# Second MoE of an attention + MoE + MoE kernel: six of eight token blocks taken in pairs, with seven products for eight

## The chip, the core and the metric

The kernel runs on one core of a Trainium2 chip, as one launch. The metric is the device time of that launch in microseconds (us). Three timed runs of the kernel before gave 904.86, 905.05 and 905.75 us; their median, 905.05 us, is the time to compare with.

## What is computed

Gated linear attention over 4 batches, 8 heads, 768 steps, then a MoE with a SiLU gate, then a second MoE with a maximum over three products. All arrays are float32.

```python
def _moe2_ref(x, w1, w2, w3, w_out) -> np.ndarray:      # x: 3072 tokens x 384; w1..w3: 384 x 768; w_out: 768 x 384
    h = np.maximum(np.maximum(x @ w1, x @ w2), x @ w3)
    return (h @ w_out).astype(np.float32)

def reference(**kwargs):
...
    attn_out = _attn_ref(**attn_kwargs)
    B, H, S, D = attn_out.shape
    x = np.ascontiguousarray(attn_out.transpose(0, 2, 1, 3)).reshape(B * S, H * D)
    x = _moe_ref(x=x, **moe_kwargs)
    return _moe2_ref(x=x, **moe2_kwargs)
```

Only the second MoE (`_moe2_ref`) is computed in another way after the change.

## The kernel before

**Numbers.** Every float32 operand of a MoE product is kept as two parts, a high and a low one (names that end in h and l), and a product of two 128-row tiles is three TensorE matmuls: high by high, high by low, low by high. One matmul here has 128x128 stationary weights and 384 moving columns.

**Stages.** Attention (24 tiles of 128 tokens) is worked into the first MoE, whose output y1 goes to HBM (`y1_scr`). The second MoE reads y1 back in 8 blocks of 384 tokens (`yf`, L919), splits it (`yh` L931 on ScalarE, `yl` L934 on VectorE), and goes through 6 tiles f of the 768 hidden columns per block. One such (block, f) is a slot z, 48 in all. In a slot, `p` 0 to 2 are the products with w1, w2, w3 (L769, 9 matmuls each, into PSUM banks 3, 4, 5); ScalarE copies the first out (`cp`, L951); VectorE takes the maximum with the second and the third (`m`, L954, two instructions); the hidden tile is split into high (`hh2`, L958, ScalarE) and low (`hl2`, L962, VectorE); `s2` (L969, 9 matmuls) multiplies it with w_out into banks 0 to 2. So a slot has 36 matmuls and three VectorE instructions. After a block's six slots ScalarE copies the banks out and they are stored (`ev2`, L995, L996).

**Order.** All work of the stages is given as parts to a planner (class `Order`): a name, an engine, an estimated cost, a due time, the parts that it needs. A list schedule over these numbers sets the order in which each engine's instructions are written out; the engines then run their own lists in order and wait on semaphores. `MM` is the planner's cost of nine matmuls, for the first MoE's parts too. The weights of the second MoE (`w0h` to `w2l`, `wo2h`, `wo2l`) are fetched and split during the end of the first MoE and the start of the second.

In the printed code, `slots` are the (block, f) of the first MoE (gate and value products L769, second product L816), and `wvh`, `wvl`, `woh`, `wol` are its weights, which the second MoE no longer needs.

## Time and profile before

| | us |
|---|---|
| median of three timed runs | 905.05 |
| the profiled execution's own time | 905.86 |
| its span, first to last instruction | 903.7 |
| TensorE (PE) busy | 886.8 (98%) |
| VectorE (DVE) busy | 530.5 (59%) |
| ScalarE (ACT) busy | 350.4 (39%) |
| second MoE, from its first product to the last matmul | 589.7 to 897.3 |

The profiled execution took 2.2 us more than its span, and is 0.81 us over the median. PE is TensorE's matmuls, PEld its weight loads (beside them), DVE VectorE, ACT ScalarE, SP the queue that issues the DMAs. Matmuls are pipelined: each is shown some 0.34 us long while the next begins after about half of that.

### The profile page before, as it was taken

What the parts mean: (1) busy time and instruction counts of PE and PEld (TensorE: products, weight loads), DVE (VectorE), ACT (ScalarE), POOL (GpSimd) and SP (SyncE); (2) the same over time, 40 slices, a digit from 0 to 9 for tenths busy, and PEclk for the clock granted to TensorE, in tenths of its full rate; (3) what the DMA queues carried; (4) which work ended last, traced back from release to release, by engine and by line L of the source; (5) the groups of instructions that cost most, each with busy time, mean ns of one, the idle gap of its engine ahead of it and who ended that gap; (6) DMA issues with size and microseconds to landing.
All of it is one profiled execution on the core that took longest, in us unless ns stands there. A gap on an engine that the chain in (4) does not pass through costs nothing.

```text
span 903.7 us, 16408 instructions
## 1 busy us (share of the span) xinstructions
PE 886.8 (98%) x6527; PEld 864.9 (96%) x6527; DVE 530.5 (59%) x1063; ACT 350.4 (39%) x898; POOL 22.5 (2%) x66
## 2 busy tenths in 40 slices
PE   7999999999999999999999999999999999999997
PEld 6889999999999999999999999999999999999996
DVE  8999999987666666666663377483332323323221
ACT  4578775333333223233233277561221212212121
POOL 1000000000000000000000000000000000000000
PEclk9999999999999999999999999999999999999999
DMA  9845654343223223223201145140110100101000
GB/s 196 190 114 159 193 168 131 101 123 84 58 57 85 57 58 84 58 58 81 61 10 45 36 131 164 39 140 17 37 53 1 53 27 27 53 1 53 1 27 30
DMA packets 106243, 69.17 MB, mean 77 GB/s; under 512 B 49200, under 2 KB 103856, under 8 KB 106160
## 3 DMA queue, kind: packets, MB, share of 16 engines
...
q14 instruction: 30, 0.25, 0.1%
...
## 4 chain that ended last, share of the span: by engine, by line
PE 89%; DVE 4%; DMA 3%; SPq 2%; ACT 1%; issue 1%; DVEq 0%; ACTq 0%
PE bank L769 56%; PE bank L816 15%; PE bank L969 8%; PE bank L653 2%; PE bank L691 2%; PE bank L685 2%; DMA raw<-in_moe_w_val_dram 1%; PE bank L676 1%; DVE cv_t L59 1%; DVE cv_t L60 1%; SPq L551 1%; PE bank L776 1%; PE bank L725 1%; SPq L562 1%; PE bank L646 1%
## 5 line engine op out<-in xcount | busy, mean ns | idle before, releaser
L954 DVE TENSOR_TENSOR sg<-sg,bank 128x384 f32<-128x384 f32 x96 | 53.2, 554 | 173.0 <-PE bank L769 172.7
L802 DVE TENSOR_TENSOR sg<-sg,bank 128x384 f32<-128x384 f32 x96 | 52.8, 550 | 94.5 <-PE bank L769 93.1
L806 ACT ACTIVATE hh<-sg 128x384 fp32r<-128x384 f32 x96 | 50.0, 520 | 134.4 <-DVE sg L802 134.3
L769 PE MATMUL bank<-xh,wgh 128*128 128x384 f32 x288 | 100.7, 350 | 0.0
L816 PE MATMUL bank<-hh,woh 128*128 128x384 f32 x288 | 98.3, 341 | 0.0
L769 PE MATMUL bank<-xl,wgh 128*128 128x384 f32 x288 | 97.2, 337 | 1.2 <-DVE xl L736 1.2
L816 PE MATMUL bank<-hl,woh 128*128 128x384 f32 x288 | 96.9, 336 | 1.3 <-DVE hl L810 1.3
L769 PE MATMUL bank<-xh,wgl 128*128 128x384 f32 x288 | 97.3, 338 | 0.1
L769 PE MATMUL bank<-xh,wvh 128*128 128x384 f32 x288 | 97.0, 337 | 0.0
L769 PE MATMUL bank<-xh,wvl 128*128 128x384 f32 x288 | 96.5, 335 | 0.0
L816 PE MATMUL bank<-hh,wol 128*128 128x384 f32 x288 | 96.4, 335 | 0.0
L769 PE MATMUL bank<-xl,wvh 128*128 128x384 f32 x288 | 96.3, 334 | 0.0
L958 ACT ACTIVATE hh<-sg 128x384 fp32r<-128x384 f32 x48 | 25.2, 525 | 160.0 <-DVE sg L954 160.0
L810 DVE TENSOR_TENSOR hl<-sg,hh 128x384 fp32r<-128x384 f32 x96 | 53.3, 555 | 31.3 <-ACT hh L806 31.3
L799 ACT ACTIVATE sg<-bank 128x384 f32<-128x384 f32 x96 | 46.7, 487 | 52.3 <-PE bank L769 51.3
L816 PEld LDWEIGHTS bank<-hl,woh 128*128 128x128 f32 x288 | 54.3, 188 | 2.4 <-DVE hl L810 2.3
L816 PEld LDWEIGHTS bank<-hh,woh 128*128 128x128 f32 x288 | 54.2, 188 | 1.8
L769 PEld LDWEIGHTS bank<-xl,wgh 128*128 128x128 f32 x288 | 54.5, 189 | 1.5 <-DVE xl L736 1.5
L769 PEld LDWEIGHTS bank<-xh,wgh 128*128 128x128 f32 x288 | 54.4, 189 | 1.5
L769 PEld LDWEIGHTS bank<-xh,wgl 128*128 128x128 f32 x288 | 54.5, 189 | 0.5 <-DVE wgl L380 0.5
L769 PEld LDWEIGHTS bank<-xh,wvh 128*128 128x128 f32 x288 | 54.1, 188 | 0.5 <-DVE sg L802 0.3
L816 PEld LDWEIGHTS bank<-hh,wol 128*128 128x128 f32 x288 | 54.2, 188 | 0.0
...
## 6 DMA issues: line engine op xcount, KB each, us to landing
...
```

What stands on the lines that cost most here:

```text
L653: nc.tensor.matmul(self.sc[i][:, pr, :], self.kT[lo:hi, pr, :], self.qT[lo:hi, pr, :], start=True, stop=True)
L685: nc.tensor.matmul(self.y[tk, 2 * pr:2 * pr + 2, :].rearrange("p a d -> p (a d)"), self.qT[:, pr, tk], Sds[self.s][:, pr, :], start=True, ...
L691: nc.tensor.matmul(self.y[tk, 2 * pr + i, :], at[i][:, pr, tk], vt[:, 2 * pr + i, :], start=not self.c, stop=True, skip_group_check=True,)
L769: nc.tensor.matmul(ps, w_[:, kt, col], m_[:, kt, :], start=i == 0, stop=i == 3 * KT - 1)
L799: nc.scalar.activation(hid[s], banks[3][:, :NB], AF.Silu)
L802: nc.vector.tensor_tensor(hid[s], hid[s], banks[4][:, :NB], ALU.mult)
L806: nc.scalar.activation(hi_[s], hid[s], AF.Copy)
L810: nc.vector.tensor_tensor(lo_[s], hid.pop(s), hi_[s].bitcast(F32), ALU.subtract)
L816: nc.tensor.matmul(banks[e][:, :NB], w_[:, f, es], m_, start=f == f0 and i == 0, stop=f == f1 - 1 and i == 2)
L954: nc.vector.tensor_tensor(hid2[z], hid2[z], banks[3 + j][:, :NB], ALU.max)
L958: nc.scalar.activation(hi2[z], hid2[z], AF.Copy)
L969: nc.tensor.matmul(banks[t][:, :DM], l_[:, tsl], r_[:, f, :], start=f == 0 and i == 0, stop=f == NF2 - 1 and i == 2)
```

## The change

Blocks 0 and 1 of the second MoE stay as they were (12 slots). Blocks 2 to 7 are taken in three pairs. For a pair, a weight matrix j and two neighbouring f tiles, the hidden tiles (two f by two blocks) are a 2x2 product of tiles over three inner tiles of 128. Over inner tiles 0 and 1 that is eight products of tiles; the changed code forms sums of tiles and takes seven (a Strassen scheme). Inner tile 2 is done plainly (four products). A pair has nine such steps k (three f pairs by three j), each with seven groups X1 to X7 on PE, of 3, 3, 6, 6, 3, 6 and 6 matmuls. Groups accumulate onto what an earlier group left in the same bank, after VectorE or ScalarE has read it.

Added around the steps: nine sets of weight sums, made once on VectorE and ScalarE while blocks 0 and 1 run (`sr`, `sc`, `sh`, `sl`, then `fr`, `fh`, `fl`); four sums of y1 tiles for each pair (`t`, with splits `th`, `tl`) beside the splits of both blocks (`xh`, `xl`); in a step a copy `cp` (ScalarE), the sums `q`, `r`, and `v` 3, 2, 1 and the maxima `m` 0 to 3 (VectorE). X6 and X7 of a step are written into the next step. The hidden tiles of the pair are all kept (`hh`, `hl`), and the second product follows as parts W for six token tiles: first 12 matmuls each over the first four f, then 6 each over the last two; X6 and X7 of the last step stand behind the first W. The second product's count of matmuls does not change. Both y1 blocks of the next pair are fetched when X7 of the last step is done.

`MM` goes from 1.47 to 1.565. The core of the diff:

```diff
+    MM = 1.565
 
...
-    for blk in range(NBLK):
+
+    PLAIN = 2
+    NZ = PLAIN * NF2
+    for blk in range(PLAIN):
...
         plan.add(("s2", z), "PE", MM, due + 1.2, [("hl2", z), wts2.ready(index2["o", f]),
+                 ("X2", "sb", 1, 0) if z == NZ - 1 else None,
                  ("s2", z - 1) if z else ("s", NS - 1)] +
...
+    def whole_again(n):
+        fp, j = divmod(n, 3)
+        both = slice(2 * fp * P, 2 * (fp + 1) * P)
+        whole[n] = rt[0].tile([P, KT, 2, P], F32, name="raw", bufs=3)
+        h_, l_ = (w_[:, :, both].bitcast(F32) for w_ in w2s[j])
+        nc.vector.tensor_tensor(whole[n].rearrange("p k i f -> p k (i f)"), h_, l_, ALU.add)
+
+    def combine(n):
+        a, t = whole.pop(n), rt[0].tile([P, 5, P], F32, name="raw", bufs=3)
+        five[n] = t
+        nc.vector.tensor_tensor(t[:, 0], a[:, 0, 1], a[:, 1, 1], ALU.add)
+        nc.vector.tensor_tensor(t[:, 1], t[:, 0], a[:, 0, 0], ALU.subtract)
+        nc.vector.tensor_tensor(t[:, 2], a[:, 0, 0], a[:, 0, 1], ALU.subtract)
+        nc.vector.tensor_tensor(t[:, 3], a[:, 1, 0], t[:, 1], ALU.subtract)
+        nc.vector.tensor_tensor(t[:, 4], a[:, 2, 0], a[:, 2, 1], ALU.subtract)
+
+    def sums_high(n):
+        if not sums:
+            sums[0] = left.tile([P, KT, F1], F32R, name="wvh")
+            sums[1] = left.tile([P, KT, F1], F32R, name="wvl")
+            sums["first"] = lts[0].tile([P, 3, 2, P], F32R, name="first")
...
+        nc.vector.tensor_tensor(sum_views(n, 1), five.pop(n)[:, 1:5], sum_views(n, 0).bitcast(F32), ALU.subtract)
+
...
+    for n in range(NS1):
+        fp, j = divmod(n, 3)
+        at = NS + 3 + 0.5 * n
+        ready = [("w2", "rest", (len(chunks2) - 1) // 2 * 2), ("sl", n - 1) if n else None]
+        plan.add(("sr", n), "DVE", 1.1, at, ready, partial(whole_again, n))
+        plan.add(("sc", n), "DVE", 1.15, at, [("sr", n)], partial(combine, n))
+        plan.add(("sh", n), "ACT", 0.7, at, [("sc", n), ("s", NS - 1)], partial(sums_high, n))
+        plan.add(("sl", n), "DVE", 0.85, at + 0.05, [("sh", n)], partial(sums_low, n))
...
+        last_use = [("p", NF2 + 2 * fp + 1, j)] if fp < 2 else []
+        at = NS + 10.5 + 0.1 * n
+        plan.add(("fr", n), "DVE", 0.65, at, [("sl", NS1 - 1)] + last_use, partial(first_again, n))
...
+    def three(ps, w_, x_, start):
+
+        for i, (l, r) in enumerate(((w_[0], x_[0]), (w_[0], x_[1]), (w_[1], x_[0]))):
+            nc.tensor.matmul(ps, l, r, start=start and i == 0, stop=i == 2, skip_group_check=True)
+
+    kept = []
+    sets = (6, 7, 3), (4, 5, 0), (1, 2)
+    MM1 = MM / 3
+    last_pe = ("p", NZ - 1, 2)
+    for sb in range(1, NBLK // 2):
+        b0, b1 = 2 * sb, 2 * sb + 1
+        at0 = NS + NZ + (sb - 1) * 11.3
+        xs, T, hid3, tmp = {}, {}, {}, {}
+        A_, B_, E_ = sets
...
+        def fetch0(b0=b0, xs=xs):
+            xs["h", 0] = mp.tile([P, KT, NB], F32R, name="xh")
+            xs["l", 0] = mp.tile([P, KT, NB], F32R, name="xl")
+            nc.sync.dma_start(out=xs["l", 0].bitcast(F32), in_=y1_scr[:, :, b0 * NB:(b0 + 1) * NB])
...
+        def mixed(i, xs=xs, T=T):
+
+            b11, b21 = (xs["l", 0][:, k_, :].bitcast(F32) for k_ in (0, 1))
+            b12, b22 = (xs["f"][:, k_, :] for k_ in (0, 1))
+            T["f", i] = lts[0].tile([P, NB], F32, name="hid", bufs=7)
+            x_, y_ = {1: (b12, b11), 2: (b22, T.get(("f", 1))), 3: (b22, b12), 4: (b21, T.get(("f", 2)))}[i]
+            nc.vector.tensor_tensor(T["f", i], x_, y_, ALU.subtract)
...
+        if sb == 1:
+            free0, free1 = [("p", NF2 - 1, 2)], [("wo2 there",)]
+            free_x1, early = [("p", NZ - 1, 2)], NS + 7
+            free_t = [("sl", n) for n in range(NS1)]
...
+            free0 = free1 = free_x1 = free_t = [("X7", "sb", sb - 1, 8)]
+            early = at0 - 3
...
+        plan.add(name("yf", 0), "SP", 1.64, early, [("yst", final[0], i) for i in range(KT)] + free0, fetch0, later=2.2)
+        plan.add(name("yf", 1), "SP", 1.64, early, [("yst", final[1], i) for i in range(KT)] + free1 + [name("yf", 0)],
...
+        for i in range(1, 5):
+            plan.add(name("t", i), "DVE", 0.55, early, [name("yf", 0), name("yf", 1)] + free_t + free1, partial(mixed, i))
+            plan.add(name("th", i), "ACT", 0.5, early, [name("t", i)], partial(mixed_h, i))
...
+            def X1(ps=bank_a, w_of=w_of, x_of=x_of):
+                three(ps, w_of(0, 0), x_of(0, 0), True)
+
+            def X2(ps=bank_b, s_of=s_of, T=T):
+                three(ps, s_of(2), T[2], True)
+
+            def X3(ps=bank_c, s_of=s_of, w_of=w_of, x_of=x_of, T=T):
+                three(ps, s_of(1), T[1], True)
+                three(ps, w_of(1, 2), x_of(2, 1), False)
+
+            def X4(ps=bank_a, w_of=w_of, x_of=x_of):
+                three(ps, w_of(0, 1), x_of(1, 0), False)
+                three(ps, w_of(0, 2), x_of(2, 0), False)
+
+            def X5(ps=bank_b, s_of=s_of, T=T):
+                three(ps, s_of(3), T[3], False)
+
+            def X6(ps=bank_b, w_of=w_of, x_of=x_of, T=T):
+                three(ps, w_of(1, 1), T[4], False)
+                three(ps, w_of(1, 2), x_of(2, 0), False)
+
+            def X7(ps=bank_c, s_of=s_of, x_of=x_of):
+                three(ps, s_of(4), x_of(1, 1), False)
+                three(ps, s_of(5), x_of(2, 1), False)
...
+            x1ready = [name("xl", 1, i) for i in range(KT)]
+            pe("X1", MM1, at, old + xready + [wts2.ready(index2[j, 2 * fp]), wts2.ready(index2[j, 2 * fp + 1])], X1)
+            pe("X2", MM1, at, [name("tl", 2), ("sl", n)], X2)
+            after = [("s2", NZ - 1)] if sb == 1 and k == 0 else []
+            pe("X3", 2 * MM1, at, [name("tl", 1), ("fl", n)] + x1ready + after, X3)
+            if k:
+                for kind, cost, need, run in kept_back:
+                    pe(kind, cost, at, need, run, k=k - 1)
+            pe("X4", 2 * MM1, at, [name("cp", k)], X4)
+            pe("X5", MM1, at, [name("q", k), name("tl", 3)], X5)
+            kept_back = [("X6", 2 * MM1, [name("r", k), name("tl", 4)], X6), ("X7", 2 * MM1, [name("v", k, 3)], X7)]
...
+            plan.add(name("q", k), "DVE", 0.55, at + 0.1, [name("X2", k), name("cp", k)] +
+                     ([name("m", k - 2, 1)] if k > 1 else []), add_q)
+            plan.add(name("r", k), "DVE", 0.55, at + 0.3, [name("X5", k)] + ([name("m", k - 2, 3)] if k > 1 else []), add_r)
+            hold = [name("hl", fp - 1, i) for i in range(4)] if fp and j == 0 else []
+            plan.add(name("v", k, 3), "DVE", 0.55, at + 0.3, [name("r", k), name("X3", k)] + hold, partial(last_add, "r", bank_c, 3))
+            plan.add(name("v", k, 2), "DVE", 0.55, at + 0.9, [name("X6", k)] + hold, partial(last_add, "p", bank_b, 2))
+            plan.add(name("v", k, 1), "DVE", 0.55, at + 0.9, [name("X7", k)] + hold, partial(last_add, "q", bank_c, 1))
+            plan.add(name("m", k, 0), "DVE" if j else "ACT", 0.55, at + 0.4, [name("X4", k)] + hold +
+                     ([name("m", k - 1, 0)] if j else []), first_of)
+            for i in (3, 2, 1):
+                if j:
+                    plan.add(name("m", k, i), "DVE", 0.55, at + 0.9, [name("v", k, i), name("m", k - 1, i)], partial(most_of, i))
+                else:
...
+
+                def low(i, fp=fp, hid3=hid3):
+                    e_ = (2 * fp + i // 2) * 2 + i % 2
+                    nc.vector.tensor_tensor(
+                        stored[1][:, e_, :], hid3.pop((fp, i)), stored[0][:, e_, :].bitcast(F32), ALU.subtract
+                    )
...
+        for late in range(2):
+            for t in range(2 * TPB):
+                def second(part=late, t=t, i=out_banks[t]):
+                    wo2h, wo2l = wo2s
+                    b, tt = divmod(t, TPB)
+                    tsl = slice(tt * P, (tt + 1) * P)
+                    fs = range(4, NF2) if part else range(4)
+                    for f in fs:
+                        h_, l_ = (st[:, 2 * f + b, tsl] for st in stored)
+                        for m_, (l, r) in enumerate(((h_, wo2h), (l_, wo2h), (h_, wo2l))):
+                            nc.tensor.matmul(
+                                banks[i][:, :DM], l, r[:, f, :], start=f == 0 and m_ == 0, stop=f == NF2 - 1 and m_ == 2
...
+                    need += [name("m", 7, i) for i in range(4)] + [name("m", 8, 0)]
+                elif not late and sb == 1:
+                    need += [("ev2", PLAIN - 1, tt) for tt in range(TPB)]
+                plan.add(name("W", t, late), "PE", MM1 * (2 if late else 4), at, need + [kept[-1]], second)
...
-    plan.add("flag", "DVE", 1.5, NS + NZ - 6, [("m", NZ - 5, 1)] + [("w2", "check", i) for i in range(len(chunks2))],
+    plan.add("flag", "DVE", 1.5, NS + NZ + 20, [("W", "sb", 1, 0, 0)] + [("w2", "check", i) for i in range(len(chunks2))],
              flag)
```

**VectorE in the middle of a pair.** First the kernel before, two slots of a late block: `m`, `m`, `hl2` each.

```order
L954 TENSOR_TENSOR sg<-sg,bank_77 128x384
L954 TENSOR_TENSOR sg<-sg,bank_78 128x384
L962 TENSOR_TENSOR hl<-sg,hh 128x384
L954 TENSOR_TENSOR sg<-sg,bank_77 128x384
L954 TENSOR_TENSOR sg<-sg,bank_78 128x384
```

Then the changed kernel, second pair, around step 1: `r` and `v` 3 of step 1 (L1216, L1224), a maximum (L1230), `q` of step 2 (L1212), `v` 2 and 1 of step 1 with their maxima, `m` 0 of step 2 (L1237), `r` of step 2.

```order
L1237 TENSOR_TENSOR hid<-hid,bank_77 128x384
L1216 TENSOR_TENSOR hl<-sg,bank_78 128x384
L1224 TENSOR_TENSOR hl<-hl,bank_73 128x384
L1230 TENSOR_TENSOR hid<-hid,hl 128x384
L1212 TENSOR_TENSOR hh<-sg,bank_75 128x384
L1224 TENSOR_TENSOR sg<-sg,bank_78 128x384
L1230 TENSOR_TENSOR hid<-hid,sg 128x384
L1224 TENSOR_TENSOR hh<-hh,bank_73 128x384
L1230 TENSOR_TENSOR hid<-hid,hh 128x384
L1237 TENSOR_TENSOR hid<-hid,bank_74 128x384
L1216 TENSOR_TENSOR hl<-sg,bank_75 128x384
```

Where a slot of 36 matmuls had three VectorE instructions, a step of 33 has five (j = 0), nine (j = 1) or thirteen (j = 2, with four `hl`): 27 in three steps.

**PE at the handover from block 1 to the first pair.** Before, at the same place: the end of p 2 of a slot (w2), and then two of the next slot's products ahead of this slot's `s2`.

```order
L769 MATMUL bank_78<-xl,w2h 128x384
L769 MATMUL bank_78<-xh,w2l 128x384
L969 MATMUL bank_73<-wo2h,hh 128x384
L969 MATMUL bank_73<-wo2h,hl 128x384
L969 MATMUL bank_73<-wo2l,hh 128x384
```

(The L969 rows there are the `s2` of the slot before.) Now, with the last p 2 of block 1 in the first rows, X1 and X2 of the first step, and then the `s2` of that same slot (L972):

```order
L769 MATMUL bank_78<-xl,w2h 128x384
L769 MATMUL bank_78<-xh,w2l 128x384
L1085 MATMUL bank_79<-xh,w0h 128x384
L1085 MATMUL bank_79<-xl,w0h 128x384
L1085 MATMUL bank_79<-xh,w0l 128x384
L1085 MATMUL bank_80<-raw,wvh 128x384 x2
L1085 MATMUL bank_80<-raw,wvl 128x384
L972 MATMUL bank_73<-wo2h,hh 128x384
L972 MATMUL bank_73<-wo2h,hl 128x384
```

Six matmuls stand between a slot's last product and its own `s2`, where 27 or more stood.

**PE in the first MoE, where only `MM` differs.** Before, the transposes and scores of an attention tile (L646, L653) come right behind a second product:

```order
L816 MATMUL bank_75<-hl,woh 128x384
L816 MATMUL bank_75<-hh,wol 128x384
L646 MATMUL bank_78<-ident,kT 128x112 x4
L653 MATMUL bank_79<-qT,kT 128x128
L653 MATMUL bank_80<-qT,kT 128x128
```

Now they stand four groups of nine matmuls later, behind a value product:

```order
L769 MATMUL bank_77<-xh,wvh 128x384
L769 MATMUL bank_77<-xl,wvh 128x384
L769 MATMUL bank_77<-xh,wvl 128x384
L646 MATMUL bank_78<-ident,kT 128x112 x4
L653 MATMUL bank_79<-qT,kT 128x128
```

Up to the second MoE, PE's list differs at such places alone: this tile, one group of nine a little behind it, the parts of the next tiles up to about one tile further, and one `s2` in the first slots of the second MoE. VectorE's and ScalarE's lists differ in the same stretch, and again where the second MoE's weights are split.

## Rows read from the trace of the kernel before

**Rows 1.** The page, parts 1 and 2: busy times, tenths by slice.
```profile
PE 886.8 (98%) x6527; PEld 864.9 (96%) x6527; DVE 530.5 (59%) x1063; ACT 350.4 (39%) x898; POOL 22.5 (2%) x66
...
PE   7999999999999999999999999999999999999997
...
DVE  8999999987666666666663377483332323323221
...
PEclk9999999999999999999999999999999999999999
```
**Rows 2.** The page, part 4: the chain that ended last, by engine.
```profile
PE 89%; DVE 4%; DMA 3%; SPq 2%; ACT 1%; issue 1%; DVEq 0%; ACTq 0%
```
**Rows 3.** Windows (us, then busy and count of PE, PEld, DVE, ACT, POOL; clock).
```profile
645.38:860.40 215.02, 215.02 (x1226) 215.02 (x1225) 63.71 (x117) 47.54 (x98) 0.00 (x0) 1.00 0.09 28
```
**Rows 4.** What PE waited for, whole span: us in total, times, longest.
```profile
PE bank L816 <- DVE hl L810: 1.3, 3, 0.9
...
PE bank L769 <- DVE xl L736: 1.2, 1, 1.2
```
**Rows 5.** Groups by line in 620 to 860: busy us, mean ns, idle before.
```profile
L954 DVE TENSOR_TENSOR sg<-sg,bank 128x384 f32<-128x384 f32 x76 | 42.1, 554 | 145.1 <-PE bank L769 145.1
...
L769 PEld LDWEIGHTS bank<-xl,w2h 128*128 128x128 f32 x114 | 21.4, 188 | 0.0
...
L951 ACT ACTIVATE sg<-bank 128x384 f32<-128x384 f32 x38 | 18.7, 492 | 50.7 <-PE bank L769 50.7
L934 DVE TENSOR_TENSOR xl<-xl,xh 128x384 fp32r<-128x384 f32 x18 | 9.0, 551 | 0.0
```
**Rows 6.** Timeline of VectorE near 671 us: three instructions in a row.
```profile
671.55 1.49 DVE L934 TENSOR_TENSOR xl<-xl,xh 128x384 fp32r<-128x384 f32 x3
```
**Rows 7.** Groups of VectorE by form, other widths.
```profile
L666 DVE TENSOR_TENSOR at<-bank,mask 128x512 f32<-128x512 f32 x48 | 30.9, 684 | 15.3 <-PE bank L653 15.3
...
L626 DVE TENSOR_TENSOR Sd<-S,all 48x192 f32<-48x192 f32 x40 | 13.6, 340 | 0.3
```
**Rows 8.** Timelines of PE, DVE and ACT, 893 to 898 us.
```profile
893.53 0.34 PE L769 MATMUL bank<-xh,w2l 128*128 128x384 f32 x1
...
895.29 0.34 PE L969 MATMUL bank<-wo2h,hh 128*128 128x384 f32 x1
895.67 0.44 PE L969 MATMUL bank<-wo2h,hl 128*128 128x384 f32 x1
...
893.91 0.55 DVE L954 TENSOR_TENSOR sg<-sg,bank 128x384 f32<-128x384 f32 x1 [0.96 <-PE bank L769]
895.05 0.56 DVE L962 TENSOR_TENSOR hl<-sg,hh 128x384 fp32r<-128x384 f32 x1 [0.59 <-ACT hh L958]
...
894.50 0.53 ACT L958 ACTIVATE hh<-sg 128x384 fp32r<-128x384 f32 x1 [3.20 <-DVE sg L954]
896.32 1.56 ACT L995 ACTIVATE yo<-bank 128x384 f32<-128x384 f32 x3 [1.29 <-PE bank L969]
```
**Rows 9.** Windows: blocks 0 and 1, and a stretch of the first MoE.
```profile
589.70:666.00 76.30, 76.10 (x434) 75.75 (x433) 34.02 (x70) 26.70 (x64) 0.00 (x0) 1.00 0.18 58
...
100.00:200.00 100.00, 98.88 (x816) 95.44 (x815) 94.87 (x197) 54.89 (x152) 3.14 (x8) 1.00 0.54 147
```
**Rows 10.** DMAs: L919 to landing; two loads in flight from 589.74; rate.
```profile
DMA to landing us min/median/max: 4.2/4.5/5.0
...
589.74 0.53 SPq L919 DMA_DIRECT2D xl<-y_scr  x1
...
590.38 4.93 DMA raw<-in_moe_w_dram
...
593.70:594.70 1.00, 1.00 (x8) 1.00 (x7) 0.04 (x1) 0.48 (x2) 0.00 (x0) 1.00 1.13 393
```
**Rows 11.** Timelines of PE and DVE near 123 us, the tile of the third pair of lists.
```profile
123.08 0.55 PE L646 MATMUL bank<-ident,kT 112*128 112x112 f32 x4
123.56 1.16 PE L653 MATMUL bank<-qT,kT 48*128 48x128 f32 x16
...
125.80 1.28 DVE L666 TENSOR_TENSOR at<-bank,mask 128x512 f32<-128x512 f32 x2
```

More of the change, by code (lines that the diff above doesn't have):

```diff
@@ L770, in products @@
                 i += 1
-    MM = 1.47
+    MM = 1.565
     def fill():
@@ L859, in gla_moe_moe @@
     w2s = []
-    wo2s = []
+    wo2s, lts, stored = [], [], []
     def right():
@@ L999, in gla_moe_moe, with rows_of, sum_views, first_sum @@
                          ([] if blk else [("yst", len(passes) - 1, t)]), evacuate)
+    NS1 = 9
+    def rows_of(fp, i):
+        return cols(2 * fp + i)
+    sums = {}
+    def sum_views(n, half):
+        t = sums[half].rearrange("p k f -> p (k f)")
+        return t[:, n * 512:(n + 1) * 512].rearrange("p (s f) -> p s f", s=4)
+    def first_sum(n, half):
+        fp, j = divmod(n, 3)
+        return sums["first"][:, j, half, :] if fp == 2 else w2s[j][half][:, 0, rows_of(fp, 1)]
+    whole, five = {}, {}
@@ new lines, in sums_high, with sums_low, first_again @@
+    def sums_high(n):
[3 more added lines that the diff above has]
+            sums["first"] = lts[0].tile([P, 3, 2, P], F32R, name="first")
+        nc.scalar.activation(sum_views(n, 0), five[n][:, 1:5], AF.Copy)
+    def sums_low(n):
+        nc.vector.tensor_tensor(sum_views(n, 1), five.pop(n)[:, 1:5], sum_views(n, 0).bitcast(F32), ALU.subtract)
+    def first_again(n):
+        fp, j = divmod(n, 3)
+        f1 = rows_of(fp, 1)
+        t, u = (lts[0].tile([P, NB], F32, name="hid", bufs=7)[:, 0:P] for _ in range(2))
+        (h0, l0), (h1, l1) = ([w_[:, k_, f1].bitcast(F32) for w_ in w2s[j]] for k_ in (0, 1))
+        nc.vector.tensor_tensor(t, h0, l0, ALU.add)
+        nc.vector.tensor_tensor(u, h1, l1, ALU.add)
+        nc.vector.tensor_tensor(t, t, u, ALU.add)
+        five["first", n] = t
@@ new lines, in first_high, with first_low @@
+    def first_high(n):
+        nc.scalar.activation(first_sum(n, 0), five["first", n], AF.Copy)
+    def first_low(n):
+        nc.vector.tensor_tensor(first_sum(n, 1), five.pop(("first", n)), first_sum(n, 0).bitcast(F32), ALU.subtract)
+    for n in range(NS1):
+        fp, j = divmod(n, 3)
+        at = NS + 3 + 0.5 * n
[7 more added lines that the diff above has]
+        plan.add(("fr", n), "DVE", 0.65, at, [("sl", NS1 - 1)] + last_use, partial(first_again, n))
+        plan.add(("fh", n), "ACT", 0.3, at, [("fr", n), *last_use], partial(first_high, n))
+        plan.add(("fl", n), "DVE", 0.25, at + 0.05, [("fh", n)], partial(first_low, n))
```

122 lines of the change are left out of this document (121 added, 1 removed).

## Prediction

> **What bounds the kernel now.** I read the page's busy times and slices first: PE is busy 98% of the span, in all slices but the first and the last, at full clock, while VectorE falls from tenths of 6 and more in the first half to 2 or 3 in the second MoE [rows 1]. Next the chain that ended last: 89% of it is PE [rows 2]. Then a window over blocks 1 to 7 of the second MoE: 215.02 us, and PE is busy in all of them, at clock 1.00, with VectorE at 30% (63.71) and ScalarE at 22% [rows 3]. Last, what PE waited for: the largest entries are 1.3 and 1.2 us in the whole span [rows 4]. So the second MoE lasts as long as its matmuls do. A matmul fewer saves its pace, and work on VectorE is free until it makes PE wait.
>
> **What goes.** The pace is 215.02 us / 1226 = 0.175 us; I use 0.1757, since the window cuts a few instructions at its edges (34 slots of 36 are 1224 matmuls: 215.02 / 1224). A pair of six f by two blocks had 12 x 27 = 324 product matmuls; nine steps of 33 are 297. The second product keeps 108. So 27 go per pair, 81 in three: 81 x 0.1757 = **-14.2 us**. The Trainium skill, page "TensorE: Matmul & The Clock Gate", section "Wait — 56ns, not 53.3ns?", has back-to-back matmuls start N / 2.4 GHz + 2.5 ns apart, which is 162.5 ns for 384 columns; by that estimate 81 matmuls would give 13.2 us and the sum would end 1.0 us higher. This trace's stream is slower than that, so its own pace counts.
>
> **Steps of a pair.** PE takes 33 x 0.1757 = 5.80 us, 17.4 for three steps. VectorE has 27 instructions there. The nearest rows are maxima from a bank, 0.554 us, and splits, 0.551 [rows 5]. Three in a row take 1.49 us [rows 6], thus 0.47 from start to start ((1.49 - 0.55) / 2). One that waits for the one before costs about 0.59: 0.55 and a hop of 0.04, as from a maximum's end (893.91 + 0.55) to 894.50 where ScalarE starts on it [rows 8]. So 27 take 12.7 to 15.9 us of 17.4 (73 to 91%). All depends on staying under 17.4 / 27 = 0.645 us each. ScalarE has 8 of about 0.5 [rows 5], 4 us. The tightest chain is X5, `r`, X6, for X6 adds onto the bank that `r` reads: from the start of a product's last matmul to the reader's is 0.38 us (893.53 to 893.91 [rows 8]), with the instruction and a hop 0.97; between stand twelve matmuls (X1, X2, X3), 13 x 0.1757 = 2.28. That leaves 1.3 us, or two queued VectorE instructions. I take **0**; the ends are 0 and 27 x 0.66 - 17.4 = 0.4 us per three steps, 3.8 for nine.
>
> A rule that speaks against this: the Trainium skill, "VectorE: DVE Perf Modes", section "The DRAIN you can't avoid", says that a drain of about the duration less 266 ns follows each VectorE instruction before the next one starts. Read as time on top, 0.55 + 0.28 would be 22.5 us for 27, over by 5.1 in three steps, 46 in all, and the kernel much slower. The row of three in 1.49 us excludes that reading for instructions that do not depend on each other; no row here has a long alternation of sums and maxima.
>
> **Ends of pairs.** X7 of step 8 frees the fetch of the next pair. From there to the next X1 stand 96 matmuls (5 x 12 + 6 x 6), 16.9 us. The chain under them: two loads of y1. One load lands after 4.5 us; two loads in flight from 589.74 were done at 595.31 (590.38 + 4.93), 5.6 us, and these are 192 KB more, 0.5 us at the 393 GB/s of that stretch [rows 10]: 6.1. Then four sums `t`, each at most 0.59 (2.4), four `tl` at 0.47 (1.9), three `xl` (1.4), hops through ScalarE 0.6: 12.4 us. 4.5 us are spare: **0**, and a load late by more than that shows one for one, twice.
>
> **Blocks 0 and 1.** VectorE is busy 34.0 of 76.3 us there [rows 9]. A set of weight sums is one instruction 768 wide, nine of 128, one of 512. A 512 wide one takes 0.684, a 192 wide one 0.340 [rows 7]; the line through them gives 0.95 for 768 and 0.29 for 128. So a set is 0.95 + 9 x 0.29 + 0.68 = 4.2, nine are 38 us; 14 of 0.55 prepare the first pair (7.7). With full durations 79.9 us of 76.3, 105%; with 0.08 less for each of 183 if none waits (start to start), 65, 85%. VectorE idles ahead of nearly every maximum now, 145.1 us in 76 [rows 5], 1.9 each, and the sums fill that. I take **0**, near the lower end since each instruction here is mostly queued behind another; the upper end is 3.6 us.
>
> **Handover.** Before, `s2` of a slot had 27 and more matmuls between itself and its own products. The last `s2` of block 1 has six (X1, X2). The end of the kernel before shows the bare chain: last product at 893.53, maximum at 893.91, `hh` at 894.50, `hl` at 895.05, the matmul that reads `hl` at 895.67 [rows 8]: 2.14 us. The six matmuls and the first of `s2` give it (1 + 6 + 1) x 0.1757 = 1.41. So 0.73 us at least; with two queued `xh` copies of ScalarE ahead of `hh` (2 x 0.49) and two `xl` ahead of `hl` (2 x 0.47) 2.65. What stands behind the waiting matmul is all of PE's list, X3 of the first step first, and nothing covers it. I take **+1.2**: the bare chain and one copy. In exchange the same chain at the end of the kernel, where `s2` stood right behind it (0.38 between the two matmuls in place of 0.18 [rows 8]), is gone, since W of four tiles stands there: **-0.2**. The evacuation and the store behind the last matmul stay.
>
> **First MoE.** `MM` moves four attention groups on PE. A tile's transposes now start four groups (36 matmuls, 6.3 us) later; they were at 123.08, its scores at 123.56, its mask on VectorE at 125.80 [rows 11]. VectorE is busy 94.87 of 100 us in that stage, PE 98.88 [rows 9], so VectorE has little room to catch up a delay and PE's next products may wait for its splits. No row prices this. From below: 0 (a gain of up to 1.1, which PE lost in 100 us, is possible). From above: three places, each losing the longest such wait of before, 1.2 [rows 4], 3.5. I take the middle, **+1.7**, as both engines are nearly full there.
>
> **Sum.** -14.2 + 1.2 - 0.2 + 1.7 = -11.5 us. Span 903.7 - 11.5 = 892.2; the profiled execution took 2.2 more, and is 0.81 over the median: 892.2 + 2.2 - 0.8 = **893.6 us**.
>
> **Rivals.** (a) VectorE is somewhat slower than I read, because in the steps nearly every instruction reads what the last one wrote: at 0.66 us each three steps lose 0.4 us, and a few queued instructions eat the 1.3 us of X6 in the j = 2 steps, say 0.3 in each of 27 groups, 3.8 + 8 x 0.3 = 6 us: 900, range 897 to 903. For it: 91% at the upper duration. Against: the 27 are not one chain, q of one step stands between v and m of another. Chance 0.10. (b) The re-planned first MoE or the blocks with the weight sums cost their upper ends, 3.5 - 1.7 and 3.6, together 5 us: 899. Against: PE never waited over 1.2 us in a stage with VectorE at 95%. Chance 0.10. (c) **Slower**: VectorE becomes the bound of the steps. From 17.4 + 11.5 / 9 = 18.7 us for 27 instructions, 0.69 us each, it eats everything; at 0.72 each the three steps take 19.4, nine times 2.0 = 18 us lost: 911. It would take 0.13 us more between dependent instructions than the hop that I read. Chance 0.05. The drain of the Trainium skill's VectorE page ("VectorE: DVE Perf Modes") as time on top, 893.6 + 46 = 940, is the far end of (c); the row of three in 1.49 leaves it next to nothing of that chance. (d) The change doesn't do what it says: a bank or a buffer is freed so late that PE waits in each step what it saves (three matmuls, 0.53 us): 27 x 0.53 = 14.2, and the time is 905 to 908, within 0.2% for its lower part. The 1.3 us of slack speaks against it. Chance 0.05. (e) The early moves cost nothing or gain up to 1.1 and the handover is bare: 893.6 - 1.7 - 0.5 - 1.1 = 890.3 at best; this belongs to the forecast's own range, 890 to 896.5.
>
> **How the numbers follow.** The forecast has 0.70, (a) and (b) 0.10 each, (c) and (d) 0.05 each. The range of 8 in 10 reaches from (e), 889.8, over the forecast to 898, where about half of (a) and (b) begins; what is beyond, 0.2, is the rest of these, (c), (d). A measurement of this kernel tells about 0.2%, 1.8 us, from no change: 903.2 to 906.9 counts as the same. Faster: 0.70 + 0.20 + a bit of (d) = 0.91; the same 0.03 (the lower part of (d)); slower 0.06.
>
> **What would show it.** A step of 33 matmuls should last 5.80 us and a pair, from X1 to the next pair's X1, 405 x 0.1757 = 71.2, with PE busy all through. PE's list of waits should have one new entry at `s2` (the split hidden tile) of 0.7 to 2.7 us, and none at X1, X4 or X6. VectorE in a pair should be busy 73 to 91% of the steps; where its groups show over 0.6 us, (a) or (c) holds. The stretch from 100 to 200 us shows the early cost as PE's idle time, by a later start of the second MoE. A wait of X1 for the splits at a pair's start would prove the loads late. I am wrong if the steps run above 6.0 us, or the second MoE starts over 4 us later.

## The result, and the profile after

The changed kernel takes 892.62 us (median of four runs, 892.18 to 892.83) where the kernel before, timed beside it, takes 905.34 (904.86 to 905.75): a ratio of 0.9859, interval 0.9842 to 0.9876. The forecast was 893.6, the range 889.8 to 898. The profiled execution's span is 891.0 us, against 903.7.

First the page, busy times and slices, then the first line of the chain (columns as in [rows 1] and [rows 2]).

```profile
PE 871.4 (98%) x6446; PEld 848.2 (95%) x6446; DVE 639.5 (72%) x1321; ACT 363.6 (41%) x928; POOL 22.1 (2%) x66
...
PE   7999899999999999999999999999999999999996
...
DVE  8999999997666666666665367559886874865780
...
PE 86%; DVE 6%; DMA 3%; ACT 2%; SPq 2%; issue 1%; DVEq 0%; ACTq 0%
```

PE has exactly 81 matmuls fewer (6527 - 6446) and is still the bound; VectorE has 258 instructions more and fills the second half of the span: in the slices of the pairs it has 4 to 8 tenths (the last slice apart), where it had 2 or 3.

What PE waited for, whole span (us in total, times, longest; compare [rows 4]):

```profile
...
PE bank L769 <- ACT sg L799: 1.5, 1, 1.5
...
PE bank L816 <- DVE hl L810: 1.2, 1, 1.2
...
PE bank L972 <- ACT hh L961: 0.4, 1, 0.4
PE bank L972 <- DVE hl L965: 0.3, 1, 0.3
```

The entry left out ahead of them is at the start of the program (L579, 4.0 us; 4.3 in the kernel before). No step of a pair is in the list (L1085 and L1313 are absent). New are a wait in the first MoE (L769 for ScalarE) and the two of the handover (L972).

Windows: blocks 0 and 1 to the first X1; the nine steps of the second pair up to the last X5; the 96 matmuls of W behind the pair's last X7 (columns as in [rows 3], then the share of the DMA engines and GB/s).

```profile
591.00:668.72 77.72, 77.72 (x442) 77.33 (x442) 68.19 (x176) 36.22 (x85) 0.00 (x0) 1.00 0.19 64
...
742.37:792.16 49.79, 49.79 (x285) 49.79 (x285) 35.78 (x70) 10.20 (x21) 0.00 (x0) 1.00 0.03 9
796.51:812.98 16.47, 16.47 (x96) 16.47 (x96) 9.19 (x19) 7.88 (x17) 0.00 (x0) 1.00 0.36 115
```

VectorE is at 88% in blocks 0 and 1 (68.19 of 77.72) and 72% in the steps. The granted clock is 1.00 in all three. One matmul takes 49.79 / 284 = 0.1753 us in the steps, 16.47 / 95 = 0.1734 in W; it was 0.1757 [rows 3].

To see where the time went, each trace is cut at four matmuls, by their starts in the timeline of PE: the first gate product of the first MoE, the first product of the second MoE, the first X1 (before: the first product of block 2), the last matmul; and the span's end.

| stretch, us | before | after | difference |
|---|---|---|---|
| start to first gate product | 49.25 | 49.00 | -0.25 |
| first MoE, to first product of the second | 540.46 | 542.00 | +1.54 |
| blocks 0 and 1 | 77.93 | 77.72 | -0.21 |
| from there to the last matmul's start | 229.36 | 215.05 | -14.31 |
| behind it | 6.73 | 7.20 | +0.47 |
| span | 903.7 | 891.0 | -12.76 |

### The profile page after: what moved, and what is told of

Read it like the earlier page. It is cut to its first block, busy times and chain, and to the rows that moved or that the text cites. A ratio compares the mean times of both kernels' runs of the same rounds, so it can differ in the third digit from the quotient of the medians.

```text
span 891.0 us, 16476 instructions
## 1 busy us (share of the span) xinstructions
PE 871.4 (98%) x6446; PEld 848.2 (95%) x6446; DVE 639.5 (72%) x1321; ACT 363.6 (41%) x928; POOL 22.1 (2%) x66
## 4 chain that ended last, share of the span: by engine, by line
PE 86%; DVE 6%; DMA 3%; ACT 2%; SPq 2%; issue 1%; DVEq 0%; ACTq 0%
PE bank L769 35%; PE bank L1085 17%; PE bank L816 15%; PE bank L1313 6%; PE bank L653 2%; PE bank L691 2%; PE bank L776 2%; PE bank L972 2%; DMA raw<-in_moe_w_out_dram 1%; PE bank L685 1%; PE bank L676 1%; PE bank L725 1%; SPq L562 1%; DVE cv_t L59 1%; SPq L551 1%
## 5 line engine op out<-in xcount | busy, mean ns | idle before, releaser
L802 DVE TENSOR_TENSOR sg<-sg,bank 128x384 f32<-128x384 f32 x96 | 53.0, 552 | 95.7 <-PE bank L769 95.1
L806 ACT ACTIVATE hh<-sg 128x384 fp32r<-128x384 f32 x96 | 50.0, 521 | 149.0 <-DVE sg L802 148.9
L769 PE MATMUL bank<-xh,wgh 128*128 128x384 f32 x288 | 100.7, 349 | 1.5 <-ACT sg L799 1.5
L769 PE MATMUL bank<-xl,wgh 128*128 128x384 f32 x288 | 96.7, 336 | 1.2 <-DVE xl L736 1.2
L769 PE MATMUL bank<-xh,wgl 128*128 128x384 f32 x288 | 96.9, 336 | 0.2 <-DVE wgl L380 0.2
L769 PE MATMUL bank<-xh,wvh 128*128 128x384 f32 x288 | 96.7, 336 | 0.0
L769 PE MATMUL bank<-xh,wvl 128*128 128x384 f32 x288 | 96.4, 335 | 0.0
L769 PE MATMUL bank<-xl,wvh 128*128 128x384 f32 x288 | 96.2, 334 | 0.0
L799 ACT ACTIVATE sg<-bank 128x384 f32<-128x384 f32 x96 | 46.7, 486 | 38.0 <-PE bank L769 36.9
L769 PEld LDWEIGHTS bank<-xh,wgh 128*128 128x128 f32 x288 | 54.1, 188 | 3.4 <-ACT sg L799 1.8
L769 PEld LDWEIGHTS bank<-xl,wgh 128*128 128x128 f32 x288 | 54.2, 188 | 1.5 <-DVE xl L736 1.5
L769 PEld LDWEIGHTS bank<-xh,wgl 128*128 128x128 f32 x288 | 54.1, 188 | 0.9 <-DVE wgl L380 0.9
L769 PEld LDWEIGHTS bank<-xh,wvh 128*128 128x128 f32 x288 | 54.1, 188 | 0.5 <-DVE sg L802 0.5
L769 PEld LDWEIGHTS bank<-xl,wvh 128*128 128x128 f32 x288 | 54.1, 188 | 0.0
L769 PEld LDWEIGHTS bank<-xh,wvl 128*128 128x128 f32 x288 | 54.1, 188 | 0.0
```

The lines of the kernel that those rows point to most:

```text
L769: nc.tensor.matmul(ps, w_[:, kt, col], m_[:, kt, :], start=i == 0, stop=i == 3 * KT - 1)
L799: nc.scalar.activation(hid[s], banks[3][:, :NB], AF.Silu)
L802: nc.vector.tensor_tensor(hid[s], hid[s], banks[4][:, :NB], ALU.mult)
L806: nc.scalar.activation(hi_[s], hid[s], AF.Copy)
```

## The experiments

Twelve runs in four lots; in each lot the kernels shared a chip with runs of the kernel before, at 906.16 (first to fourth), 906.08 (fifth to eighth), 906.18 (ninth to eleventh) and 906.04 us (twelfth). Medians are compared by their difference to that kernel; such a difference is sure to between 1.1 and 2.0 us (the intervals of the ratios reach 0.0012 to 0.0022 to either side), so small effects are read from the stretches of the traces. A trace is one execution, too: the two of the changed kernel (after and run 5) differ by 1.2 us in the first MoE, 0.6 in blocks 0 and 1, 0.02 from X1 to the last matmul and 0.24 behind it.

| kernel | time, us | less the kernel before | first MoE | blocks 0, 1 | X1 to last | behind |
|---|---|---|---|---|---|---|
| before | 905.34 | | 540.46 | 77.93 | 229.36 | 6.73 |
| after | 892.62 | -12.7 | 542.00 | 77.72 | 215.05 | 7.20 |
| 1 after, MM 1.47 | 892.47 | -13.7 | 540.40 | 78.77 | 215.57 | 6.77 |
| 2 before, MM 1.565 | 909.61 | +3.5 | 541.31 | 78.14 | 230.94 | 6.75 |
| 3 s2 later | 892.49 | -13.7 | 542.99 | 78.34 | 213.85 | 6.72 |
| 4 last evacuations | 892.63 | -13.5 | 542.63 | 78.11 | 215.05 | 5.38 |
| 5 after again | 894.35 | -11.7 | 543.20 | 78.30 | 215.07 | 6.96 |
| 6 both, 3 and 4 | 891.76 | -14.3 | 541.36 | 78.19 | 213.82 | 5.31 |
| 7 maxima of j = 2 twice | 900.46 | -5.6 | 541.88 | 78.37 | 221.07 | 7.40 |
| 8 maxima of j = 1, 2 twice | 909.37 | +3.3 | 542.35 | 77.93 | 230.85 | 7.28 |
| 9 two pairs | 898.73 | -7.5 | 540.96 | 153.87 | 144.15 | 6.97 |
| 10 both, MM 1.47 | 891.46 | -14.7 | 540.90 | 78.93 | 215.31 | 5.45 |
| 11 both again | 891.28 | -14.9 | 541.76 | 78.18 | 213.83 | 5.57 |
| 12 tenth, sums later | 888.86 | -17.2 | 539.58 | 78.54 | 213.75 | 5.28 |

**1. The re-plan undone (first run).**

```diff
-    MM = 1.565
+    MM = 1.47
```

> The changed kernel with MM at 1.47: PE's order up to the second MoE is that of the kernel before again. Theory: the re-planned order of the first MoE costs what the later start of the second MoE shows (591.0 against 589.7 us). Then the first product of the second MoE is back near 589.7, the 1.5 us wait of a gate product for ScalarE near 105 us is gone, and the time is 891.3, 1.3 under the changed kernel. Rival: the late start comes from DMA times at the program's beginning, not from the order; then the time stays 892.6.

The theory holds for the first MoE, which is back at 540.40 us without the wait near 105 us, but the gain does not reach the end: the span falls by 0.3 us. Against the kernel before the median is 1.0 us lower than the first of the changed kernel, which lies within what such a difference is sure to. 1.05 us came back in blocks 0 and 1 (0.6 against 78.1, the mean of the eight traces of changed kernels with the order of 1.565 and two plain blocks) and half a us at the handover, where the waits grew:

```profile
PE bank L972 <- DVE hl L965: 0.9, 1, 0.9
PE bank L972 <- ACT hh L961: 0.4, 1, 0.4
PE bank L769 <- DVE sg L957: 0.2, 1, 0.2
```

PE came to the second MoE earlier, counted from the first gate product, and found VectorE not ready. But MM also changes VectorE's own order in blocks 0 and 1 (the two maxima of a slot then stand together behind a set of weight sums, from 645.53), and no run separates the two causes. Runs 10 and 12 take that up.

**2. The re-plan alone, in the kernel before.** The same line, the other way.

> The kernel before with MM at 1.565 and nothing else. Theory: the re-plan alone costs 1.3 us, so 906.6. Rival: nothing, 905.3. A third: the order at 1.565 is better in the kernel before and was spoiled by something else, under 904.5.

It is 3.5 us slower. Of this the first MoE shows 0.85; 1.6 lie at the kernel's end. There the new cost also moved the `s2` of the slot before the last ahead of the last product, so that nothing covers the last slot's `s2`: its first matmul starts at 898.10, 1.53 us behind the last product, with an entry of 1.2 us for ScalarE's `hh` (L958). The changed kernel does not have this wait. So the run confirms the sign in the first MoE, and its size only with the others: over ten profiles with the order of 1.565 (after, runs 2 to 9 and 11) that stretch is 541.0 to 543.2, mean 542.0; over four with the order of 1.47 (before, runs 1, 10, 12) 539.6 to 540.9, mean 540.3. The re-plan costs 1.7 us there.

**3. The handover.** The second product of the slot before the last goes behind the last p 2:

```diff
-                 ("X2", "sb", 1, 0) if z == NZ - 1 else None,
+                 ("X2", "sb", 1, 0) if z == NZ - 1 else ("p", NZ - 1, 2) if z == NZ - 2 else None,
```

> The second product of the slot before the last of block 1 is put behind the last product p 2, so that 15 matmuls (in place of 6) stand between that product and its own s2. Theory: the handover costs 1.18 us as a bare dependency chain of 2.6 us under 1.41 us of matmuls; with (1+9+6+1) x 0.1757 = 2.99 us of cover both waits vanish: 891.4. Rival: the wait only moves, to X3 of the first step, which needs the splits that are made at the same time (xl of the second block until 671.6): 892.2 to 892.6.

In the changed kernel the chain was this (timelines of PE, DVE, ACT at the handover; last product, X2's last matmul, `s2`; the last maximum and `hl`; copies of the first pair and `hh`):

```profile
668.55 0.34 PE L769 MATMUL bank<-xh,w2l 128*128 128x384 f32 x1
...
669.61 0.34 PE L1085 MATMUL bank<-raw,wvl 128*128 128x384 f32 x1
670.38 0.45 PE L972 MATMUL bank<-wo2h,hh 128*128 128x384 f32 x1 [0.43 <-ACT hh L961]
671.14 0.44 PE L972 MATMUL bank<-wo2h,hl 128*128 128x384 f32 x1 [0.32 <-DVE hl L965]
...
668.92 0.56 DVE L957 TENSOR_TENSOR sg<-sg,bank 128x384 f32<-128x384 f32 x1
...
669.59 1.02 DVE L1136 TENSOR_TENSOR xl<-stg,xh 128x384 fp32r<-128x384 f32 x2
670.53 0.55 DVE L965 TENSOR_TENSOR hl<-sg,hh 128x384 fp32r<-128x384 f32 x1
...
668.99 0.92 ACT L1132 ACTIVATE xh<-stg 128x384 fp32r<-128x384 f32 x2
669.82 0.51 ACT L961 ACTIVATE hh<-sg 128x384 fp32r<-128x384 f32 x1
```

From product to the matmul on `hl` 2.59 us (671.14 - 668.55): the 2.14 of [rows 8] and 0.45 more. Of this some 0.31 lie ahead of `hh`, behind the two copies (maximum to `hh` 0.90, where it was 0.59), and 0.16 ahead of `hl`, behind two `xl` on VectorE (`hh` to `hl` 0.71, where it was 0.55). Starts are 0.77 and 0.76 us apart where 0.18 is the pace, so 1.18 lost. In the third run X1 to the last matmul falls by 1.20 us, and PE shows no wait there:

```profile
671.03 0.34 PE L1085 MATMUL bank<-raw,wvl 128*128 128x384 f32 x1
671.21 0.34 PE L972 MATMUL bank<-wo2h,hh 128*128 128x384 f32 x1
671.39 0.41 PE L972 MATMUL bank<-wo2h,hl 128*128 128x384 f32 x1
```

The rival, a wait moved to X3, does not appear. The median of the run could not show it: its first MoE was 1.0 us longer than that of the first profile, 0.7 of it in the same wait for ScalarE near 105 us (2.25 us in place of 1.52). Runs 6 and 11 do.

**4. The last evacuation.**

```diff
-                    o = mp.tile([P, DM], F32, name="yo", bufs=3)
+                    o = mp.tile([P, DM], F32, name="sg") if b0 == NBLK - 2 and t > 3 else mp.tile([P, DM], F32, name="yo", bufs=3)
```

> The last two evacuations of the last pair write to other tiles (sg) than the three of yo. Theory: the last evacuation waits 1.5 us too long (885.67 in place of 884.15) for the store that frees its yo tile, so the time falls by 1.5 to 891.1. Rival: the stores themselves set the end, one after the other, and the last one lands when it did: 892.6; halfway if the six stores share a rate.

The changed kernel's ScalarE at the end, fifth and sixth evacuation:

```profile
883.15 0.49 ACT L1320 ACTIVATE yo<-bank 128x384 f32<-128x384 f32 x1 [0.55 <-PE bank L1313]
885.67 0.49 ACT L1320 ACTIVATE yo<-bank 128x384 f32<-128x384 f32 x1 [2.03 <-DMA out_dram<-yo]
```

The last matmul starts at 883.77, and its evacuation 1.90 us later: the sixth tile, with three buffers for six, waits for a store. In the fourth run it waits for PE alone, 0.37 us behind the last matmul (885.06):

```profile
885.43 0.49 ACT L1320 ACTIVATE sg<-bank 128x384 f32<-128x384 f32 x1 [0.55 <-PE bank L1313]
```

Behind the last matmul 5.38 us are left of 7.20. In the table the seven traces of changed kernels without this edit have 6.72 to 7.40 there, the five with it 5.28 to 5.57. That is the theory; the median of this run alone, with a first MoE 0.6 us longer, does not show it.

**5 and 6. The changed kernel again, and both edits.**

> The changed kernel itself once more, beside the next three, as their measure: 892.6, 12.7 under the kernel before; from its first gate product to the first product of the second MoE 542.0 to 543.0 us, as in the three profiles with that order so far.

> The later second product and the other tiles for the last evacuations, both in one. Theory: the profiles of the two edits showed 1.2 us less between the first X1 and the last matmul, and 1.8 us less behind the last matmul, and the two are in series: 3.0 us under the changed kernel, 889.6. Rival: no more than the better one of them, 891, because the medians of each alone moved by less than its profile.

On one chip 894.35 and 891.76, 2.6 us apart, and 3.6 by the ratios (0.9870 and 0.9830); the two stretches together give 1.25 + 1.65 = 2.9. The effects are in series, as the theory says. The eleventh run repeats the kernel: 891.28.

> The same kernel as the sixth run (both edits, MM at 1.565), to stand beside the run with MM at 1.47 on one chip: 3.0 us under the changed kernel, 889.6.

**7 and 8. How much VectorE has to spare in the steps.** The maxima are issued twice, in the steps j = 2, or j = 1 and 2 (and likewise `m` 0):

```diff
-                nc.vector.tensor_tensor(h_, h_, tmp.pop(("v", k, slot)), ALU.max)
+                v_ = tmp.pop(("v", k, slot))
+                for _ in range(2 if k % 3 in (2,) else 1):
+                    nc.vector.tensor_tensor(h_, h_, v_, ALU.max)
```

> The four maxima of every j = 2 step are issued twice (same result): 31 VectorE instructions in three steps in place of 27, the added ones each waiting for the one before. Theory: VectorE is busy 37.55 of 52.80 us in a pair now, 0.51 each; four more at 0.59 make 16.3 of 17.4 us per three steps, which is still under: 892.6 to 893.5. Rival: the order, not the sum, is what is short; a j = 2 step already has thirteen, with four more 17 x 0.55 = 9.4 us against 5.8, and the backlog reaches the next step's r: 1 us per three steps, 900 or more.

> The maxima of the j = 1 and j = 2 steps are issued twice: 35 instructions in three steps. Theory: 13.9 + 8 x 0.59 = 18.6 us against 17.4, so VectorE becomes the bound and each three steps lose 1.2 us: 892.6 + 9 x 1.2 = 903.5, near the kernel before. Rival: only the pace of three in a row counts, 35 x 0.47 = 16.5, and the time stays 892.6.

Run 7 goes to the rival. X1 to the last matmul grows by 6.0 us: six steps (from X6 to X6) of 6.65 us, each followed by one of 5.90, where the others have 5.75 to 5.79: 6 x (0.86 + 0.11) = 5.8. PE's new entry is X6 for `r` (L1216), six times:

```profile
PE bank L1085 <- DVE hl L1216: 4.3, 6, 0.7
```

In the changed kernel `r` ends between 1.33 and 1.37 us ahead of X6 in all 27 steps; here is one step (DVE, then PE; X6 starts with `cv_t`):

```profile
757.84 0.55 DVE L1216 TENSOR_TENSOR hl<-sg,bank 128x384 f32<-128x384 f32 x1
...
759.76 0.51 PE L1085 MATMUL bank<-cv_t,w2h 128*128 128x384 f32 x2
```

759.76 - (757.84 + 0.55) = 1.37. With the doubled maxima `r` of the step that follows stands behind them:

```profile
692.59 0.55 DVE L1224 TENSOR_TENSOR sg<-sg,bank 128x384 f32<-128x384 f32 x1
693.17 1.15 DVE L1232 TENSOR_TENSOR hid<-hid,sg 128x384 f32<-128x384 f32 x2
694.24 0.55 DVE L1224 TENSOR_TENSOR hh<-hh,bank 128x384 f32<-128x384 f32 x1
694.83 1.15 DVE L1232 TENSOR_TENSOR hid<-hid,hh 128x384 f32<-128x384 f32 x2
695.89 0.55 DVE L1291 TENSOR_TENSOR wol<-hid,woh 128x384 fp32r<-128x384 f32 x1
696.36 0.55 DVE L1216 TENSOR_TENSOR hl<-sg,bank 128x384 f32<-128x384 f32 x1
...
695.93 0.34 PE L1085 MATMUL bank<-xh,w1l 128*128 128x384 f32 x1
696.96 0.62 PE L1085 MATMUL bank<-cv_t,w0h 128*128 128x384 f32 x2 [0.69 <-DVE hl L1216]
```

There is no idle time among these VectorE rows. VectorE's backlog is worked off in the next step, in which it idles again. Over three steps VectorE had time left; within one it had not. The changed kernel's own trace shows why: from X6 to X6, three steps in a row have VectorE busy 5.69, 3.44 and 4.67 us of 5.8 (the rows give PE, PEld, DVE), so the fullest step had 0.1 us left.

```profile
759.76:765.55 5.79, 5.79 (x34) 5.79 (x34) 5.69 (x12) 2.30 (x5) 0.00 (x0) 1.00 0.00 1
765.55:771.34 5.79, 5.79 (x34) 5.79 (x34) 3.44 (x8) 0.49 (x1) 0.00 (x0) 1.00 0.00 0
771.35:777.12 5.77, 5.77 (x34) 5.77 (x34) 4.67 (x10) 1.06 (x3) 0.00 (x0) 1.00 0.01 3
```

In run 8 `r` is late in five steps of nine (15 in three pairs; 6 waits for a `v` of 0.3 us come on top):

```profile
PE bank L1085 <- DVE hl L1216: 8.2, 15, 0.8
```

X1 to the last matmul is 15.8 us longer, and the kernel is slower than before. That is more than the sum over three steps gives (11), and VectorE still idles in one step of three (busy 4.73 of 5.91 us from 773.70 to 779.61), so here too the queue of single steps binds and not the sum. With maxima as the added work, the turn from gain to loss lies between 31 and 35 instructions in three steps.

**9. Two pairs in place of three.** `PLAIN = 4`, the pairs from block 4 on, and the fetch and the due times of the first pair put behind block 3 likewise.

```diff
-    PLAIN = 2
+    PLAIN = 4
...
-    for sb in range(1, NBLK // 2):
+    SB0 = PLAIN // 2
+    for sb in range(SB0, NBLK // 2):
...
-        at0 = NS + NZ + (sb - 1) * 11.3
+        at0 = NS + NZ + (sb - SB0) * 11.3
```

> Blocks 0 to 3 plain and two pairs in place of three: 54 matmuls fewer than before instead of 81. Theory: each pair is worth its 27 matmuls, 4.74 us, and a little of pace; the handover and the first MoE cost the same: 892.6 + 4.8 to 5.2 = 897.6. Rival: the gain is not even, since the weight sums have 40 more slots' worth of matmuls to hide in, and the pair in the middle of pairs costs something at its ends: 895 to 896 or 899.

X1 to the last matmul is 70.90 us shorter, which is what a pair takes; two plain blocks add 75.75 (153.87 less 78.12, the mean of after and runs 3 to 5). So a pair is worth 4.85 us, where the theory has 4.74 and a little of pace, and the gain is even. By the medians, each against the kernel before beside it, two pairs win 7.5 us (the theory: 7.7) and three 11.7 to 12.7; such medians alone would not exclude the rival. (The plain blocks give the weight sums 12 slots more to hide in, not 40.)

**10. Both edits, with MM at 1.47.**

> The later second product and the other tiles at the end, with MM at 1.47. Theory: the order of the first MoE at 1.47 saves 1.8 us there and its run alone gave back 0.9 in blocks 0 and 1, where VectorE is late with the weight sums, and 0.5 at the handover, which the later second product hides now: about 1 us under the same kernel at 1.565, 888.8. Rival: blocks 0 and 1 end no earlier whatever the order before them, since the weight sums set their end: 889.6, the same.

The time is the rival's (891.46 beside 891.28 in run 11). In the traces the earlier order saves 0.9 us in the first MoE against run 11, and 0.75 are lost in blocks 0 and 1, 1.5 at the handover, in spite of the longer cover. (The execution that was traced took 893.20, 1.7 over the run's median.) VectorE at the end of block 1, the last two maxima (L957) of the block between weight sums:

```profile
669.73 0.29 DVE L1059 TENSOR_TENSOR hid<-hid 128x128 f32<-128x128 f32 x1
669.94 0.55 DVE L957 TENSOR_TENSOR sg<-sg,bank 128x384 f32<-128x384 f32 x1
670.40 0.29 DVE L1066 TENSOR_TENSOR w2l<-hid,w2h 128x128 fp32r<-128x128 f32 x1
670.61 0.55 DVE L957 TENSOR_TENSOR sg<-sg,bank 128x384 f32<-128x384 f32 x1
```

There is no idle time ahead of any of them. The last maximum starts at 670.61, with X1 at 670.67. Right behind its product it would start 1.4 us before X1 (nine matmuls of `s2` between product and X1, 10 x 0.1757 - 0.38); in run 3 it starts 0.8 before.

**12. The sums for X3 later.**

```diff
-        at = NS + 10.5 + 0.1 * n
+        at = NS + 10.3 + 0.85 * n
```

> The tenth run's kernel with the due times of the sums for X3 (fr, fh, fl) spread over the first pair's steps: the last three or four sets now stand behind the maxima of the last plain slot and the splits of the first pair. Theory: in the tenth run VectorE, 88% busy in blocks 0 and 1, was late with these sums, which cost 0.75 us in the blocks and 1.5 at the handover; without them the earlier start of the second MoE (540.4 to 540.9 in place of 542.2 us) reaches the end: X1 at most 78.2 us after the first product, 213.9 us from X1 to the last matmul, time 889.5 where the tenth run had 891.5. Rival: the sums only move into the first steps, where they push r back beyond its 1.35 us of slack before X6: 891 again, with waits at L1085.

888.86 us, 17.2 under the kernel before, where the changed one is 11.7 to 12.7 under it: ratio 0.9817, interval 0.9803 to 0.9830. The last maximum now starts 1.4 us ahead of X1 (667.79), and `s2` does not wait; X1 to the last matmul is 213.75:

```profile
666.40 0.56 DVE L957 TENSOR_TENSOR sg<-sg,bank 128x384 f32<-128x384 f32 x1 [0.26 <-PE bank L769]
```

Blocks 0 and 1 still take 78.54, 0.3 over the 78.2 that the theory allowed: a wait of a product for a maximum at 645.58 stays (starts 0.51 and 0.28 us apart), which runs 1 and 10 have as well and the order of 1.565 has not. (VectorE was busy 84% of blocks 0 and 1 in run 10; the 88% are the changed kernel's.) The first MoE was also the shortest of all (539.58); of the 2.4 us to run 11, 2.2 are that stretch, so the part that its own chance holds is not separated. No wait at L1085 appears, so the rival falls. But part of the margin is gone: in the three runs with MM at 1.47 (1, 10, 12) `r` ends only 0.44 to 0.47 us ahead of X6 in two steps of nine, and 1.33 to 1.37 in the others.

## Why the prediction was right

**The removed matmuls (-14.2).** Right, and 1.0 us too small. Less the handover (1.18) and the kernel before's own wait at its end, which I had put at 0.2, the stretch from X1 to the last matmul shortens by 14.31 + 1.18 - 0.2 = 15.3. 81 x 0.1757 are 14.2; the rest is pace, 0.1753 over 891 step matmuls and 0.1734 over 324 of W, where 0.1757 was the mean before. The sum had taken the old pace for all that stays. A pair takes 70.8 us from X1 to X1 (813.15 - 742.37; 71.2 forecast).

**The steps (0).** Right in the sum and in its margin: 1.3 us were worked out for X6, 1.33 to 1.37 are there. VectorE's 27 instructions take 13.80 us of 17.35 in the three steps shown under run 8, 80%, in the lower half of 73 to 91. (The 72% above is lower because that window begins with a step without maxima and leaves out the work behind the last X5.) One takes 0.51 us on average, 35.78 us for 70 in that window of 49.79, between the 0.47 of [rows 6] and the 0.55 of [rows 5]. Here the Trainium skill's drain ("VectorE: DVE Perf Modes", section "The DRAIN you can't avoid") adds no time of its own to the duration; by 0.83 us for each, the 70 would have taken 58 us, more than the window has. What the prediction had wrong is the point of decision of its rival (c), 0.69 us each over three steps: by runs 7 and 8 the limit is the queue of one j = 2 step, the 1.3 us ahead of X6 and what is in front of `r`, and it binds well before the sum does. In the sum of (a), 0.3 us in each of 27 groups would be 8.1 us; the 8 x 0.3 that stands there counts eight groups.

**Ends of pairs (0).** Right: 4.5 us of spare were forecast, and the last `xl` of the second pair ends at 737.0, 5.4 us ahead of X1 at 742.37.

**Blocks 0 and 1 (0).** Right for this kernel (77.72 against 77.93), VectorE at 68.19 us near the lower end of 65 to 80. The eight traces with this order and two plain blocks spread from 77.72 to 78.37. But the zero holds by little: runs 1 and 10, with the order of 1.47, lose 0.6 to 0.8 us there and 0.5 and 1.5 at the handover.

**Handover (+1.2).** 1.18, through the copies and the `xl` that the prediction named: not one of them whole, but a part of both queues (0.31 and 0.16 us over the bare chain). The -0.2 at the end is right too, or a little small: before, the wait and the matmul behind it lost 0.3 (895.29, 895.67, 895.94); now no W starts over 0.175 us behind the matmul ahead of it.

**The end, "stays".** Wrong: +0.47, and +0.3 as the mean of the seven traces without the edit of run 4. Two things changed. Six evacuations share three buffers, and the sixth waits 2.03 us for a store; it starts 1.90 us behind the last matmul, where the third of before started 0.38 behind it (897.39). A block's three evacuations had a buffer each; a pair's six do not. Against these 1.5 us, 1.0 are won: the last store is now issued as its evacuation ends (886.16), while before, with three evacuations in a row, it was issued 0.96 us after that (897.88). First the kernel before, then the changed one:

```profile
898.84 0.38 SPq L996 DMA_DIRECT2D out_dram<-yo  x1
...
886.18 0.33 SPq L1321 DMA_DIRECT2D out_dram<-yo  x1
```

**First MoE (+1.7).** Measured +1.54 in the first pair of profiles and 1.7 over fourteen. The size is right by luck: it was the middle of a range that no row priced, and the reason is not the one given. I expected the moved attention groups of PE to make VectorE late. But PE's list is the same up to 123 us, and the loss comes before that, from ScalarE's list. There the copy `sg` of a gate product (L799) moved from in front of a check of weights (L389, L392) to behind it, and that check waits for the load of its weights, which ends near 103.9 in both kernels. First before, then after, with PE's next gate product last:

```profile
102.53 0.49 ACT L799 ACTIVATE sg<-bank 128x384 f32<-128x384 f32 x1 [1.51 <-PE bank L769]
103.95 0.56 ACT L389 ACTIVATE junk<-raw 128x384 bf16<-128x384 f32 x1 [0.93 <-DMA raw<-in_moe_w_out_dram]
...
103.95 0.56 ACT L389 ACTIVATE junk<-raw 128x384 bf16<-128x384 f32 x1 [3.89 <-DMA raw<-in_moe_w_out_dram]
...
105.25 0.51 ACT L806 ACTIVATE hh<-sg 128x384 fp32r<-128x384 f32 x1
105.66 0.47 ACT L799 ACTIVATE sg<-bank 128x384 f32<-128x384 f32 x1
...
104.32 0.34 PE L769 MATMUL bank<-xh,wvl 128*128 128x384 f32 x1
106.18 0.45 PE L769 MATMUL bank<-xh,wgh 128*128 128x384 f32 x1 [1.52 <-ACT sg L799]
```

The two PE starts are 1.86 us apart where 0.17 is the pace, so 1.69 are lost. All ten traces with the order of 1.565 have this wait, 0.5 to 2.2 us, each 2.4 us less than ScalarE waited for that load (2.9 to 4.6); the four with the order of 1.47 have none. So the size of the term goes with when a load lands.

The terms' errors (-1.0 pace, +0.5 end, -0.2 blocks, -0.25 start, -0.2 first MoE) add up to the 1.2 us between the forecast span of 892.2 and 891.0.

Three slips in the working change nothing in the sum. The largest of PE's waits before was not 1.3 us: 4.3 us at the program's start (L579) stand ahead of the entries of [rows 4]. Three waits of 1.2 us are 3.6, not 3.5. The line through the two widths gives 0.27 us for 128 columns, not 0.29; the changed kernel shows 0.28 to 0.29.
